# One written-out list of work replaced by another, from segment 0's attention on, on one Trainium2 core

## The chip, the core and the metric

The kernel runs on one core of one Trainium2 chip. Five engines work side by side, each through its own queue in order: TensorE (PE; its weight loads are listed as PEld), VectorE (DVE), ScalarE (ACT), GpSimd (POOL) and SyncE (SP), which here only issues DMAs. They wait for one another through semaphores. ScalarE can issue DMAs too; its transfers appear as queue q10, those of SP as q1. Both share the core's 16 DMA engines. The metric is the device time of one execution in microseconds (us).

## What is computed

Sequence 2048, width 640, 32 heads of 20, in bfloat16. A memory-augmented attention layer over 4 segments of 512 tokens, then a dense layer:

```python
for s in range(4):                              # q, k, v from layernorm(x) @ wq, wk, wv
    p = softmax(qs @ ks.T * scale + causal)     # inside the segment
    a_dot = p @ vs
    a_mem = (phi(qs) @ M) / (phi(qs) @ z + 1e-6)   # phi(t) = t + 1 if t > 0 else exp(t)
    outs.append(g * a_mem + (1 - g) * a_dot)    # g = sigmoid(beta), per head
    M, z = M + phi(ks).T @ vs, z + sum(phi(ks))
h = x + concat(outs) @ wo
out = h + silu(layernorm(h) @ w1) @ w2          # w1: 640 x 1728
```

## The kernel before

Every piece of work is a named task of a few instructions on one engine. `ORDER` is one long string that lists all tasks; nothing is decided when the program runs. Going through it, `Graph.schedule` appends each task to its engine's queue. So the string fixes three things: the order on each engine, the engine where a task has a choice (`/A` ScalarE, `/D` VectorE, `/G` GpSimd, `/S` SP; for a DMA, which queue issues it) and, behind the colon, the slot of each buffer that the task takes (for PSUM the first of its banks, 0 to 7).

```python
        for row in ORDER:
            name, _, slots = row.partition(":")
            name, _, eng = name.partition("/")
```

The waits follow from that: `Tracker.add` makes an instruction wait for the last writer and readers of what it reads and overwrites, PSUM banks and buffer slots among them. A task that gets a slot waits until its former user has been read.

The tasks, with `s` the segment (0 to 3), `b` the block of 128 tokens (0 to 15), `c` a chunk of 128 rows, `f` a chunk of the 1728 (0 to 13):

- `x`, `w_...`: loads. `w_w2_0` to `w_w2_3` are four parts of w2 (L582), which land on memory that holds segment 0's q and k until its scores are done. `x12` loads blocks 12 to 15 (L579, 640 KB) into the place of blocks 0 to 3, after these have been stored. `out{b}` stores a block (L1259).
- `n1_st`, `n1_r`, `n1_ap`, `n1_tr` and `n2_...`: layer norm statistics (L747, L750), the power for the deviation (L762 or L765, then L768), its application (L774, VectorE) and the DMA transpose of the result (L798, SP), before the attention (`n1`) and before the dense layer (`n2`).
- `pr{s}{c}{w}` (L861, PE): q (w = 0) and k (w = 1), evicted from PSUM by `qe` (L869 on ScalarE, L870 on VectorE); `ex`, `pha`, `phb` make phi (L876, L883, L889). `v{s}{i}` (L826) and `ve` (L836, L837): v. `vt`: small DMAs (L901) that gather the heads that lie across chunks.
- `qk` (L938): scores of four heads. `e` (L949, ScalarE): their exponentials, two banks each. `mk` (L960, GpSimd): the mask. `av` (L981): times v. `oe` (L994 or L996): its eviction. `tn` (L1010, L1014): the memory's part and the transposition of `oe`. `nm` (three instructions L1041 to L1047, or L1027 and L1029 in segment 0): division, reading the bank of `tn`. `ad` (L1055, GpSimd): the sum. In segments 1 to 3 the tasks of a group of four heads carry the number 8 s + g; in segment 0 `x` and `y` are the first and second half of the segment's rows.
- `kt{s}{c}` (L1095, SP): DMA transpose of phi(k) out of one of three slots of phiK into one of two of phiKt. `mz` (L1103): the update of M. `ma`, `mb` (L1129, L1132, L1139): its accumulation and masked copy.
- `ot` (L1156, SP transpose), `wo` (L1164), `rs` (L1172, VectorE): output projection. `h1_{s}_{f}` (L1199; the last chunk L1193), `th` (L1208, ScalarE), `s{s}_{f}` (L1214, VectorE): the first dense matrix and silu. `h2_{b}_{part}` (L1241), `o{b}` (L1254): the second.

The dense layer of a segment is spread between the attention tasks of the next, so TensorE has matmuls to do while exponentials are made. SP's queue is in order like the others: a transfer that waits holds all behind it.

Of the kernel before, what the change touches and what calls it, by code (L numbers as in the profile page):

```python
# [389 lines left out]
w_w2_2/S w_w2_3/S phb100 tn5y:1 e7yb0:0 e7yb2 qe140/D nm5y:1 mk7yb_0 ex121:2 mk7yb_256 pha140:0 h1_0_1_0:2 th0_1_0:1  # L390
s0_1_0 qk8a0:3 pr111:7 e8a0:2 phb121 qe111/D vt16/S:0 vt10/S tn4y:0 nm4y:3 e8a2 mk8a_0 vt19/S vt13/S h1_0_8_0:1
th0_8_0:1 ex140:0 s0_8_0 h1_0_6_0:2 th0_6_0:0 phb140 qk8e0:4 e8e0:6 s0_6_0 av6y:3 oe6y/D:0 e8e2 mk8e_0 av7y:1 mk8e_256
h1_0_10_0:0 th0_10_0:1 qk8b0:2 e8b2:4 tn6y:6 oe7y/D:1 nm6y:0 tn7y:7 nm7y:3 pr130:1 ot3 ot2 s0_10_0 e8b0 mk8b_0
mk8b_384 qk9a0:4 qe130/D:0 e9a0:0 pr131:0 qe131/D vt18/S vt14/S n1_tr8:0 vt111/S e9a2 vt15/S mk9a_0 vt11/S n1_tr10
vt12/S pha130:0 vt17/S h1_0_2_0:1 qk9b0:2 h1_0_11_0:0 th0_2_0:1 mz04:6 s0_2_0 e9b0:5 e9b2 kt12:1 ma04/D:1 pha131:1
mk9b_0 mk9b_384 n1_tr9 th0_11_0:0 mz03:7 ma03/D:4 h1_0_0_0:1 th0_0_0:1 h1_0_13_0:3 mb03:0 ex130:0 qk10a0:4 s0_11_0
s0_0_0 e10a2:3 th0_13_0:0 e10a0 mb04:0 mk10a_0 s0_13_0 h1_0_9_0:2 th0_9_0:0 s0_9_0 ex131:1 phb131 phb130 h2_0_0:0
h2_0_1 kt13:0 n1_tr11 qk10b0:3 e10b0:1 e10b2 mk10b_0 mk10b_384 ex141:1 av9:7 av8:2 oe8/D:1 oe9/D:0 h2_0_2 qk10e0:2
e10e0:4 h2_0_3 o0 pha111:0 out0/S vt110/S e10e2 mk10e_0 mk10e_256 ex110:2 h2_1_0:6 phb110 qk11a0:2 e11a0:6 wo3:0 rs3
e11a2 mk11a_0 n2_st3:1 n2_r3/G h2_1_1 qk11b0:2 e11b2:0 e11b0 mk11b_0 mk11b_384 tn8:0 nm8:2,1 h2_1_2 h2_1_3 o1 qk12a0:2  # L400
out1/S n2_ap3:0 pha141:1 n2_tr3 e12a2:5 e12a0 mk12a_0 ex111:0 phb141 ad8:0 wo2:0 rs2 av10:6 oe10/D:1 qk12b0:2 mz13:7
ma13 e12b2:2 e12b0 mk12b_0 mk12b_384 phb111 n2_st2:7 pr220:1 qe220/D:0 n2_r2/D qk13a0:4 e13a2:3 av11:0 e13a0 mk13a_0
tn9:2 v20:6 kt10:0 nm9:1,0 ad9 mz12:1 ma12 oe11/A:0 n2_ap2:2 n2_tr2 ve20/A:0 qk12e0:2 e12e0:0 mz10:0 ma10 e12e2
mk12e_0 v21:6 ve21/D qk13b0:0 e13b0:1 e13b2 mk13b_0 kt11:0 kt14:1 mk12e_256 mk13b_384 pr211:5 qe211/D:0 ex211:2
pr210:4 qk14a0:0 e14a0:4 qe210/D tn11:6 pr231:5 e14a2 mk14a_0 nm11:3,1 ad11 ex210:0 qe231/D:0 ex231:1 pr200:4 qk14b0:0
e14b0:6 qe200/D:0 pha211:2 phb211 e14b2 av13:7 oe13/D:0 v23:5 ve23/A mk14b_0 mk14b_384 h1_0_8_1:4 th0_8_1:1 s0_8_1
qk14e0:0 e14e0:1 tn13:5 nm13:3,1 pr201:7 e14e2 mk14e_0 mz11:4 mk14e_256 tn10:0 ma11 qe201/A ex200:2 nm10:0,0 ad10
pha200:0 h1_0_7_1:3 th0_7_1:0 qk15a0:4 s0_7_1 pr221:2 e15a2:3 e15a0 mk15a_0 pha201:1 phb200 av14:1 oe14/D:0 qe221/A
pha221:0 ex201:2 ad13 av12:0 qk15b0:3 vt23/S:0 vt26/S vt29/S e15b2:4 e15b0 mk15b_0 tn14:1 mb11:0 mk15b_384 oe12/D:1
nm14:3,0 ad14 mb10:0 pha210:0 phb201 pr241:7 qe241/A:0 h1_0_12_1:6 th0_12_1:1 qk16b0:0 tn12:4 s0_12_1 nm12:0,1 e16b0:2  # L410
h1_0_4_1:7 th0_4_1:0 s0_4_1 e16b2 phb210 vt20/S h1_0_0_1:6 th0_0_1:1 ad12 h1_0_10_1:0 th0_10_1:0 av15:1 oe15/A:0
s0_10_1 s0_0_1 mk16b_0 ex221:2 phb221 kt22:0 qk16a0:2 mk16b_384 e16a2:6 h1_0_6_1:7 tn15:0 mb13:0 pr240:6 nm15:0,0 ad15
ot6:0 qe240/D e16a0 th0_6_1:0 ot7 ot4 ot5 s0_6_1 mb12:0 mk16a_0 h1_0_5_1:4 th0_5_1:1 qk16e0:0 e16e0:5 s0_5_1 pr230:5
qe230/D vt22/S vt27/S vt21/S pha240:0 vt25/S pha230:0 vt28/S e16e2 mk16e_0 ex240:2 vt211/S mk16e_256 v22:6 ve22/D
pha220:0 ex230:0 qk17b0:2 e17b2:3 e17b0 mk17b_0 mk17b_384 phb230 phb240 vt210/S vt24/S h1_0_13_1:1 th0_13_1:1 pha231:0
phb231 s0_13_1 h1_0_11_1:0 th0_11_1:0 ex220:0 wo6:6 qk18b0:2 e18b0:0 rs6 e18b2 mk18b_0 mk18b_384 s0_11_1 av16:1
oe16/D:1 wo7:6 phb220 ex241:2 qk17a0:0 rs7 n2_st6:6 n2_r6/G wo4:4 rs4 e17a0:6 e17a2 mk17a_0 n2_st7:4 n2_r7/G
h1_0_3_1:7 th0_3_1:0 h1_0_9_1:6 th0_9_1:1 s0_9_1 qk18e0:0 e18e0:1 wo5:4 e18e2 mk18e_0 mk18e_256 s0_3_1 n2_ap6:2 rs5
h1_0_1_1:6 th0_1_1:0 s0_1_1 h1_0_2_1:1 th0_2_1:1 s0_2_1 n2_st4:3 n2_r4/D n2_st5:0 n2_tr6:0 n2_ap7:0 n2_tr7 n2_r5/D
# [5 lines left out]
e20a2 mk20a_0 n1_st12:0 th1_12_0:0 s1_12_0 th1_1_0:1 s1_1_0 n1_r12/G n1_ap12:1 n1_tr12:0 n1_st13:3 n1_r13/G mz23:3
kt21:1 qk20e0:4 e20e0:4 h1_1_5_0:2 ma23 e20e2 th1_5_0:1 s1_5_0 n1_st14:6 n1_r14/G n1_ap13:0 n1_tr13 mk20e_0 mk20e_256
h1_1_11_0:0 qk21a0:4 th1_11_0:0 s1_11_0 e21a2:1 h1_1_2_0:1 th1_2_0:1 s1_2_0 n1_st15:1 e21a0 mk21a_0 n1_r15/D n1_ap14:2
n1_tr14 n1_ap15:3 n1_tr15 h1_1_6_0:3 th1_6_0:0 s1_6_0 h1_1_8_0:2 th1_8_0:1 qk22a0:4 e22a2:2 e22a0 v30:0 h1_1_0_0:6
s1_8_0 av21:7 ve30/A:1 th1_0_0:0 s1_0_0 oe21/A:1 av20:5 qk22b0:1 mz21:0 ma21 e22b0:3 tn21:6 nm21:1,1 ad21 mk22a_0
e22b2 mk22b_0 mk22b_384 oe20/D:1 h1_1_9_0:0 th1_9_0:1 s1_9_0 qk23a0:1 e23a2:6 v32:6 e23a0 pr300:5 qe300/A:0 qk22e0:0  # L430
e22e0:1 ve32/D mk23a_0 e22e2 mk22e_0 mk22e_256 ex300:2 kt20:1 pha300:0 tn19:6 nm19:2,0 pr310:4 qe310/D:0 ex310:1
pr301:5 mz20:7 ma20 phb300 qk23b0:0 e23b0:0 e23b2 mb20:0 ad19 kt24:1 qe301/D mk23b_0 mk23b_384 pr311:6 h1_1_3_0:4
th1_3_0:0 qe311/D qk24e0:0 e24e2:4 tn20:5 nm20:1,1 pr320:7 e24e0 ad20 qe320/A:0 ex320:2 s1_3_0 pr330:3 qe330/D:0
av23:2 qk25a0:4 e25a2:5 e25a0 mk25a_0 ex330:0 v33:0 pr321:3 qe321/A vt33/S:0 vt36/S vt30/S vt39/S oe23/D:0 qk24b0:4
e24b0:0 ve33/D tn23:0 e24b2 mk24b_0 mb23:0 mk24b_384 nm23:1,0 ad23 mk24e_0 pha330:0 mk24e_256 phb330 pha320:0 phb320
pr341:2 qe341/A:0 av22:3 qk24a0:4 e24a0:6 e24a2 mk24a_0 oe22/D:1 pr331:1 pr340:0 qe340/A qe331/D vt37/S vt35/S vt31/S
vt34/S qk26b0:4 e26b2:1 tn22:2 nm22:3,1 ad22 mb21:0 e26b0 ot11:0 ot9 vt38/S vt310/A pha340:0 ex340:2 vt311/S ot8 ot10
vt32/S v31:0 mz24:6 qk25b0:2 ve31/D e25b0:2 ma24 e25b2 mk25b_0 mk25b_384 mk26b_0 mb24:0 mk26b_384 phb340 pha310:0
# [878 lines left out]
```

## Time and profile before

| | us |
|---|---|
| median of 3 runs (302.9 to 304.97) | 304.0 |
| the profiled execution | 303.38 |
| its span, first to last instruction | 301.7 |
| TensorE busy in the span | 290.1 |
| ScalarE, VectorE, GpSimd busy | 222.4, 219.5, 141.0 |

The profile comes from one execution, whose span lies 1.7 us under its own time. A line of the profile names the line of the kernel (L1103), the tiles written and read, and a count; lines of waits name the engine that stood, what ended the wait, its sum, count and longest. Since tasks have few lines between them, a task is found in the trace by its place in its engine's order: the n-th instruction of an engine is the n-th that the list puts there. So `kt23`, the twelfth of the 15 `kt` in SP's order, is the twelfth transpose of L1095 in the trace.

### The profile page before, as it was taken

The numbers are of one execution on the slowest core, as the hardware profiler recorded it, in microseconds if no ns is written. First come the engines' busy times: TensorE is split into PE (matmuls) and PEld (weight loads), VectorE is DVE, ScalarE is ACT, GpSimd is POOL, SyncE is SP. The second block draws the span as 40 slices with busy tenths as digits, with TensorE's granted clock in tenths as the row PEclk, the third lists the DMA queues.
The fourth block names the chain that finished last, engine by engine and source line by source line (L and its number), as shares of the span: only waits on it lengthen the run. The fifth ranks groups of instructions, "written<-read, shape, count | busy, mean of one in ns | idle before, by whom it ended". The sixth has DMA issues, their size and how long they took to land.

```text
span 301.7 us, 7526 instructions
## 1 busy us (share of the span) xinstructions
PE 290.1 (96%) x3006; PEld 173.1 (57%) x3029; DVE 219.5 (73%) x517; ACT 222.4 (74%) x317; POOL 141.0 (47%) x271
## 2 busy tenths in 40 slices
...
GB/s 249 365 340 100 110 122 111 89 78 130 81 88 94 57 2 28 54 83 37 87 128 39 72 13 20 39 77 82 49 65 24 2 43 46 74 100 2 0 30 59
DMA packets 49250, 24.66 MB, mean 82 GB/s; under 512 B 39168, under 2 KB 47616, under 8 KB 49216
## 3 DMA queue, kind: packets, MB, share of 16 engines
...
q8 instruction: 24, 0.39, 0.6%
q14 instruction: 10, 0.08, 0.1%
...
## 4 chain that ended last, share of the span: by engine, by line
PE 75%; DVE 9%; DMA 7%; ACT 6%; issue 1%; POOL 0%; ACTq 0%; DVEq 0%
PE ps_all L1241 18%; PE ps_all L1199 15%; PE ps_all L861 12%; PE ps_all L826 7%; PE ps_all L938 6%; PE ps_all L1164 6%; PE ps_all L981 5%; ACT PT L949 4%; DMA phiKt<-phiK 3%; PE ps_all L1010 2%; DMA x_tok<-in_A_x_dram 2%; DVE stt L747 2%; PE ps_all L1014 1%; DMA hT<-xn_rot 1%; PE ps_all L1103 1%
## 5 line engine op out<-in xcount | busy, mean ns | idle before, releaser
L949 ACT ACTIVATE PT<-ps_all 128x1024 bf16<-128x1024 f32 (+1 forms) x168 | 157.7, 994 | 15.9 <-PE ps_all L938 14.1
L960 POOL TENSOR_SCALAR_AFFINE_SELECT PT<-PT 128x512 bf16<-128x512 bf16 x128 | 81.2, 642 | 73.2 <-ACT PT L949 70.5
L1241 PE MATMUL ps_all<-w_sb,sT 128*128 128x320 bf16 (+2 forms) x462 | 64.8, 295 | 0.0
L1199 PE MATMUL ps_all<-hT,w_sb 128*128 128x512 bf16 (+1 forms) x315 | 61.1, 336 | 1.4 <-issue 0.7
L1208 ACT ACTIVATE th<-ps_all 128x512 f32<-128x512 f32 (+2 forms) x70 | 34.8, 520 | 36.6 <-PE ps_all L1193 21.2
L1241 PEld LDWEIGHTS ps_all<-w_sb,sT 128*128 128x128 bf16 x462 | 43.2, 98 | 18.3 <-issue 2.2
L1214 DVE SCALAR_TENSOR_TENSOR sT<-th,ps_all 128x512 bf16<-128x512 f32 (+2 forms) x70 | 37.9, 560 | 18.0 <-ACT th L1208 17.4
L1199 PEld LDWEIGHTS ps_all<-hT,w_sb 128*128 128x128 bf16 x325 | 29.7, 98 | 25.5 <-issue 2.7
L1254 DVE SCALAR_TENSOR_TENSOR x_tok<-ps_all,x_tok 128x640 bf16<-128x640 f32 (+3 forms) x18 | 13.3, 748 | 22.2 <-PE ps_all L1241 22.2
L747 DVE BATCH_NORM_STATS2 stt<-x_tok 128x6 f32<-128x320 bf16 x62 | 27.2, 480 | 1.6 <-DMA x_tok<-in_A_x_dram 1.3
L768 POOL TENSOR_TENSOR rst<-rst,eps_c 128x1 f32<-128x1 f32 x32 | 18.5, 579 | 14.0 <-DVE rst L762 12.2
L1164 PE MATMUL ps_all<-wo_sb,oT 128*128 128x320 bf16 x160 | 24.1, 299 | 0.0
L1055 POOL TENSOR_TENSOR otok<-on 128x320 bf16<-128x320 bf16 x24 | 19.5, 813 | 9.6 <-DVE on L1047 9.6
L981 PE MATMUL ps_all<-PT,Vx 128*32 128x256 bf16 (+3 forms) x576 | 23.3, 287 | 0.5 <-DVE Mz L1129 0.3
L1047 DVE TENSOR_TENSOR on<-ps_all,rd 128x640 bf16<-128x640 f32 x24 | 19.8, 824 | 0.8
L996 DVE TENSOR_SCALAR oTs<-ps_all,lsc 128x512 bf16<-128x512 f32 (+1 forms) x30 | 18.3, 620 | 2.0 <-PE ps_all L981 1.9
L1164 PEld LDWEIGHTS ps_all<-wo_sb,oT 128*128 128x128 bf16 x160 | 14.9, 98 | 7.2 <-issue 2.0
L826 PE MATMUL ps_all<-wv_sb,xT 128*128 128x320 bf16 x120 | 18.3, 299 | 0.7 <-DVE sT L1214 0.3
L981 PEld LDWEIGHTS ps_all<-PT,Vx 128*32 128x32 bf16 x576 | 12.2, 96 | 10.5 <-issue 4.7
L861 PE MATMUL ps_all<-xT,wkr 128*128 128x512 bf16 x67 | 16.9, 380 | 1.0 <-issue 0.8
L861 PE MATMUL ps_all<-xT,wqr 128*128 128x512 bf16 x70 | 17.4, 380 | 0.5 <-issue 0.3
L774 DVE TENSOR_SCALAR xn_rot<-x_tok,mvt,rst 128x640 bf16<-128x640 bf16 x32 | 13.8, 438 | 5.0 <-POOL rst L768 3.8
...
## 6 DMA issues: line engine op xcount, KB each, us to landing
...
```

The source lines that it names most:

```text
L747: T.add(DV, lambda e, hh=hh: e.bn_stats(out=stt[:, s, 6 * hh:6 * hh + 6], in_=xb[:, 320 * hh:320 * hh + 320]), reads=R((xa, xsub)), writes ...
L826: fns.append(lambda e, c=c, hh=hh: e.matmul(bank(ps, hh)[:, 0:320], lhsT=xT_[:, c, 128 * i:128 * i + 128], rhs=wv_sb[:, c, 320 * hh:320 * ...
L861: fns = [lambda e, kc=kc: e.matmul(bank(ps)[:, lo:hi], lhsT=wt[:, kc, c, :], rhs=xT_[:, kc, lo:hi], start=(kc == 0), stop=(kc == NC - 1)) ...
L949: T.add(AC, lambda e: e.activation(out=pt[:, pta.slot, q0:q0 + 2, 0:width], in_=sc3[:, b0:b0 + 2, 0:width], func=ACT.Exp, scale=SCALE), re ...
L960: T.add(PO, lambda e: e.affine_select(out=v, in_=v, pattern=[[0, 4], [1, 128]], compare_op=ALU.is_ge, fill=0.0, base=0, channel_multiplier ...
L981: fns.append(lambda e, j=j, r=r, h=h, pa=pa, pt=pt, co=co, q0=q0, ji=ji: e.matmul(bank(po)[32 * r:32 * r + 32, q0:hi], lhsT=Vx[:, vx.slot, ...
L1047: T.add(DV, lambda e: e.tensor_tensor(out=on[:, ona.slot, :, :].rearrange("p b (x e) -> p b x e", e=DH), in0=v[:, :, :, 0:DH], in1=r2.unsq ...
L1164: fns.append(lambda e, c=c, hh=hh: e.matmul(bank(ps, hh)[:, 0:320], lhsT=oT[:, c, 128 * i:128 * i + 128], rhs=wo_sb[:, c, 320 * hh:320 * h ...
L1199: fns = [lambda e, c=c: e.matmul(bank(ps)[:, lo:hi], lhsT=w1_sb[:, c, 128 * f:128 * f + 128], rhs=hT[:, c, lo:hi], start=(c == 0), stop=(c ...
L1208: T.add(AC, lambda e: e.activation(out=th[:, tha.slot, lo:hi], in_=bank(ps)[:, lo:hi], func=ACT.Tanh, scale=0.5), reads=R((ps, [0])), writ ...
L1214: T.add(DV, lambda e: e.scalar_tensor_tensor(out=sT[:, f, lo:hi], in0=th[:, tha.slot, lo:hi], scalar=1.0, in1=bank(ps)[:, lo:hi], op0=ALU. ...
L1241: fns.append(lambda e, f=f, t0=t0, fr=fr, hh=hh, n=n: e.matmul(bank(pa, hh)[:, 0:n], lhsT=sT[:, f, t0:t0 + 128], rhs=w2_sb[:, fr, c0 + 320 ...
```

## The change

The list is replaced from the task `av0y` on: the first and the last rows are shown, and those between that this text speaks of. No task is added or removed, no other line of the kernel is touched. 25 tasks change their engine or queue, among them `ve23`, `qe300`, `qe320`, `qe321`, `qe340` and `oe25` (ScalarE to VectorE), `qe330`, `qe331`, `oe24` and `oe30` (VectorE to ScalarE), and seven of the last stores (between SP and ScalarE). On TensorE about a quarter of its 410 tasks start after more or less other work than before, up to 245 us by 0.1 to 3.5 us of it; from there on whole groups change places.

The words that came with the change: the list was searched anew, with the transfers of both DMA queues counted in the order of their issue times.

```diff
-av0y:2 oe0y/D:1 mz02:3 ma02/D:3 v12:0 kt01:0 e2ya2 qk2yb0:2 e2yb0:1 ve12/D phb031 e2yb2 mk2yb_0 mk2yb_256 wo1:6 rs1
-n2_st1:5 n2_r1/G qk3ya0:0 e3ya2:3 wo0:4 mb02:0 tn0y:6 nm0y:1 e3ya0 rs0 n2_ap1:3 n2_tr1:0 av1y:7 qk4ya0:0 oe1y/D:0
-pr101:6 qe101/D:0 n2_st0:3 n2_r0/G v13:4 ve13/D e4ya2:4 w_w2_0/A e4ya0 pha101:2 ex101:2 phb101 n2_ap0:3 qk3yb0:0
...
-s0_12_0 av5y:6 mb01:0 e7ya0 h1_0_4_0:7 th0_4_0:0 s0_5_0 oe5y/D:0 qk6yb0:3 e6yb2:5 e6yb0 mk6yb_0 mk6yb_256 pr110:0
-h1_0_3_0:2 th0_3_0:1 tn3y:1 s0_4_0 kt03:0 qe110/D:0 pha110:0 nm3y:0 s0_3_0 ex100:1 av4y:7 oe4y/D:1 qk7yb0:3 pr140:0
...
-qk20b0:2 e20b0:5 mk19a_0 av19:6 oe18/D:0 tn18:0 h1_1_10_0:7 e20b2 mk20b_0 mk20b_384 nm18:2,0 mz14:2
-ma14 kt23:1 mb14:0 oe19/A:0 th1_10_0:0 ad18 s1_10_0:0 qk21b0:3 x12/A tn16:0 h1_1_7_0:2 h1_1_4_0:7 nm16:2,1 e21b2:6
+av0y:2 oe0y/D:1 mz02:3 ma02/D:3 v12:0 kt01:0 e2ya2 qk2yb0:2 e2yb0:1 ve12/D phb031 w_w2_0/A e2yb2 mk2yb_0 mb02:0
+mk2yb_256 wo1:6 qk3ya0:0 e3ya2:3 wo0:4 e3ya0 rs1 n2_st1:5 n2_r1/G tn0y:6 nm0y:1 rs0 n2_ap1:3 n2_tr1:0 av1y:7 qk4ya0:0
...
+oe5y/D:1 mz01:7 ma01/D:2 mb01:0 kt03:0 tn3y:0 nm3y:0 e7ya0 h1_0_4_0:1 qk6yb0:4 e6yb0:5 pr110:0 qe110/D:0 e6yb2 mk6yb_0
...
+o0 out0/S pha111:0 n1_tr8 mk10e_0 mk10e_256 ex111:2 phb111 h2_1_0:6 phb110 qk11a0:2 e11a2:6 wo3:0 e11a0 mk11a_0 tn8:4
+rs3 nm8:2,1 ad8:0 ex141:1 n2_st3:1 pha141:1 n2_r3/D h2_1_1 qk11b0:0 e11b2:0 e11b0 mk11b_0 mk11b_384 h2_1_2 h2_1_3 o1
...
+mk14b_0 av13:7 qe200/D:0 ex200:2 v23:4 h1_0_8_1:6 mk14a_0 oe13/D:0 ve23/D mk14b_384 th0_8_1:1 qk14e0:0 s0_8_1 mz11:7
+e14e2:1 tn13:4 e14e0 ma11 pr201:6 nm13:3,1 qe201/A mk14e_0 mk14e_256 tn10:2 nm10:0,0 ad10 pha200:0 h1_0_7_1:0
...
+qk20b0:3 e20b2:5 out3/S mk19a_0 av19:2 oe18/D:0 tn18:0 mz14:7 e20b0 nm18:2,0 ad18 h1_1_10_0:6 ma14 mk20b_0 mb14:0
+kt23:1 mk20b_384 oe19/A:0 th1_10_0:0 s1_10_0:0 tn16:4 qk21b0:0 x12/A nm16:2,1 h1_1_4_0:7 ad16 e21b0:6 e21b2 pha241:0
+h1_1_7_0:6 th1_4_0:0 s1_4_0 th1_7_0:1 s1_7_0 mk21b_0 phb241 qk20a0:2 e20a2:0 h1_1_1_0:0 e20a0 n1_st12:0 h1_1_12_0:1
+th1_1_0:1 s1_1_0 mk20a_0 th1_12_0:0 s1_12_0 n1_r12/G n1_ap12:1 n1_tr12:0 n1_st13:3 n1_r13/G qk20e0:4 h1_1_5_0:2
...
+h2_15_0_0:0 h2_15_1_0 h2_15_2_0 h2_15_3_0 o15_0 out15_0/S h2_15_2_2 h2_15_3_2 o15_2 out15_2/A
```

More of the change, by code (lines that the diff above doesn't have):

```diff
@@ L390 @@
[L390 to L419, printed above, removed]
@@ L425 @@
[L425 to L438, printed above, removed]
-phb310 h1_1_13_0:7 h2_4_0:0 h2_4_1 qk26a0:2 th1_13_0:0 s1_13_0 e26a2:3 h2_4_2 h2_4_3 av25:6 av24:7 e26a0 mk26a_0 o4
@@ new lines @@
+e4ya0:4 oe1y/D:0 pr101:6 qe101/D:0 v13:4 e4ya2 n2_st0:3 ve13/D pha101:2 ex101:2 n2_r0/G n2_ap0:3 n2_tr0 qk3yb0:0
+e3yb2:5 pr120:7 qe120/D:0 phb101 pha120:0 e3yb0 mk3yb_0 qk4yb0:2 e4yb0:0 w_w2_1/S e4yb2 mk4yb_0 mk4yb_256 mk3yb_256
+ex120:0 av2y:6 oe2y/D:1 pr100:0 qe100/D qk5ya0:2 e5ya2:2 tn2y:6 nm2y:2 pr121:1 qe121/D e5ya0 qk5yb0:4 e5yb0:6 phb120
+pha121:0 n1_ap8:3 pr141:0 e5yb2 mk5yb_0 qk6ya0:1 qe141/D:0 h1_0_7_0:5 tn1y:7 nm1y:1 e6ya0:1 th0_7_0:0 av3y:6 oe3y/D:1
+mk5yb_256 s0_7_0:0 pha100:0 e6ya2 h1_0_12_0:0 th0_12_0:0 s0_12_0 h1_0_5_0:1 th0_5_0:1 qk7ya0:2 e7ya2:3 s0_5_0 av5y:6
```

97 lines of the change are left out of this document (66 added, 31 removed).

## Prediction

> **What bounds the kernel now.** I read the page's first part, then busy time in stretches of one stage each, then TensorE's waits from 43 us on, where the two lists part, and then the DMA queues at the two largest of them.
>
> ```profile
> PE 290.1 (96%) x3006; PEld 173.1 (57%) x3029; DVE 219.5 (73%) x517; ACT 222.4 (74%) x317; POOL 141.0 (47%) x271
> ```
> ```profile
> 43.00:75.00 32.00, 29.94 (x365) 16.44 (x363) 26.72 (x67) 30.00 (x44) 12.71 (x22) 1.00 0.39 98
> 75.00:100.00 25.00, 24.63 (x295) 14.98 (x294) 17.54 (x41) 23.04 (x32) 13.99 (x23) 1.00 0.50 83
> 100.00:150.00 50.00, 49.62 (x564) 29.57 (x560) 40.14 (x94) 45.26 (x65) 28.79 (x46) 1.00 0.27 52
> 150.00:174.00 24.00, 21.91 (x206) 10.17 (x202) 19.00 (x45) 21.20 (x29) 10.13 (x18) 1.00 0.39 79
> 174.00:269.00 95.00, 93.78 (x935) 55.70 (x939) 66.58 (x132) 59.68 (x76) 43.95 (x71) 1.00 0.24 48
> ```
> The columns of the stretches are start:end, length, then busy us of PE, PEld, DVE, ACT and POOL, the granted clock, DMA share and GB/s. TensorE is full (49.62 of 50 us) except in the first and the fourth stretch, and the clock is 1.00 throughout. From 43 to 75 us ScalarE is as full as TensorE (30.00 against 29.94 of 32). Both lists hold the same matmuls, so a list can only take away TensorE's idle time, or add to it. This is that idle time from 43 us on:
>
> ```profile
> PE ps_all L861 <- issue: 1.1, 7, 0.2
> PE ps_all L1014 <- DVE oTs L996: 0.9, 1, 0.9
> PE ps_all L1199 <- issue: 0.7, 4, 0.2
> PE ps_all L938 <- DVE sT L1214: 0.5, 1, 0.5
> PE ps_all L1014 <- ACT PT L949: 0.4, 1, 0.4
> PE ps_all L1103 <- DMA phiKt<-phiK: 0.4, 1, 0.4
> PE ps_all L1199 <- DVE sT L1214: 0.3, 1, 0.3
> PE ps_all L1010 <- DVE x_tok L1254: 0.3, 1, 0.3
> PE ps_all L826 <- DVE sT L1214: 0.3, 1, 0.3
> ```
> The 1.8 us put down to "issue" are not waits: in the timeline each stands beside a group of 4 matmuls where the code has 5, a missing record. The others sum to 3.1 us, and gaps too short for this view add some 0.5. So **3.6 us, 1.2%, is all that a new list can gain**; nothing but judgement of the new waits bounds the loss.
>
> Two places make up most of it. At 54.6 us `tn2y` (L1014) waits 0.9 for `oe2y`; VectorE is late there because `n2_ap0` (L774) stood 0.84 us for a transpose, issued at 48.32 by SP and landed 4.17 us later, where the median of that line is 2.6. From 158 to 167 us four waits (0.4, 0.46, 0.34, 0.25: 1.45 us) follow from `kt23`, issued at 152.76 and landed 6.0 us later (median 2.5), for which `pha241` held VectorE 2.35 us. At both, ScalarE's queue (q10) had a 640 KB load under way: `w_w2_0`, issued at 47.51, and `x12`, issued at 152.34. The queues in the DMA view (packets, MB, share of 16 engines), first for 153 to 156 us, where no other queue is listed, then for 156 to 159:
>
> ```profile
> q10 hardware_dynamic: 411, 0.53, 66.6%
> ```
> ```profile
> q1 hardware_dynamic: 544, 0.13, 57.5%
> q10 hardware_dynamic: 117, 0.13, 11.9%
> ```
> The reader is to see that SP's queue q1 moves nothing in the first three us, though `kt23` was issued before them; its 0.13 MB flow when the load is nearly over. From 48.5 to 51 us it is the same: 484 packets of q10 and none of q1. A transpose behind a large load of the other queue waits for nearly all of it.
>
> **The change, part by part.**
>
> *`w_w2_0`* goes from behind `e4ya2` to behind `e2yb0` on ScalarE, which started at 43.26. It waits for what `e2yb0` waits for (`qk2yb0`), so it holds nothing; its issue (0.38 us of ScalarE's sequencer) is the same. With its 4.4 us to landing it is through at about 47.9, before `n2_tr1` goes out at 48.32. That transpose then lands at 48.32 + 2.6 = 50.9, `n2_ap0` waits for its own `n2_r0` instead (51.33), and the instructions up to `oe2y` (0.45 + 0.68 + 0.43 + 0.47, less overlaps, then 0.47) end near 53.7, when TensorE is there. The 0.85 us go. But ScalarE is full to 75 us: of its idle time in 53 to 60 us only 0.38, 0.12 and 0.11 can close, and at 72 us TensorE waits for an exponential (the 0.4 of L1014 <- L949), which no edit moves. Gain between 0 and 0.85; I take **0.4**, nearer to ScalarE's 0.6 less the next item.
>
> *Order within 55 to 73 us.* `tn3y` moves 2.5 us forward, next to `pr110`, which uses the same PSUM bank 0; `nm3y` (0.56 us) must empty it, behind `oe5y` and `ma01` on VectorE. By the rows' durations `nm3y` ends about 0.25 us after TensorE is ready for `pr110`. That wait is new; it costs nothing at 72 us as long as ScalarE is the later one, and is why I took 0.4.
>
> *`kt23` and `x12`.* `mz14` now precedes `h1_1_10_0`, so `kt23`, which waits for it (the slot of phiKt), goes out 1.03 us earlier, near 151.7; `x12`, dispatched behind `th1_10_0`, goes out some 0.45 later, near 152.8. The order of the two issues turns round. `kt23` should land by 151.7 + 2.5 = 154.2, before VectorE comes to `pha241` (end of `nm16`, 155.3). `mz23` is 1.6 us of TensorE work later as well. VectorE is then held by `n1_st12`, which needs `x12`: 152.8 + 4.4 (the other 640 KB load) to 5.9 (its own landing now) is 157.2 to 158.7, against 160.08 now. VectorE gains 1.4 to 2; of TensorE's 1.45, I take **1.2**; ends 0 and 1.45.
>
> *SP's order in 69 to 92 us.* SP issues without a pause there. `n1_tr8` goes from 77.58 to behind `out0`, last of its four. The transfers ahead of it end near 88.4, so it lands at about 91 to 93; `pr220`, its first reader, starts at 95.51. `kt12` goes out some 0.8 earlier. Nothing, unless it lands 2.5 us late.
>
> *`ex111`, `ex141`, `ve23`, `qe300` to `qe340`.* `ex141` (0.71) fills the 0.67 us in which ScalarE waits at 89 us, and `ex111` leaves a place where ScalarE would then wait for `qk12b0`: zero. `ve23` (0.71) goes to VectorE, into its 1.34 us of idle time before `s0_8_1`; `tn13`, now on the same banks, comes about 0.5 us after it. Of six evictions in 176 to 195 us four go to VectorE and two to ScalarE; `qe340` there ends just when `v31` wants its bank (195.27 against 195.28), as `qe331` does now. Zero, cover thin.
>
> *The end* (from 245 us) moves most, by up to 7.6 us, but TensorE runs through either order: its waits from 269 us are none, ScalarE has 7.71 busy of 33 us. The last two stores change queues; both queues issue one in 0.33 us. Zero.
>
> *New waits elsewhere*, not visible in this trace: from 0 to the 1.1 us that the present list has outside the two places (0.4, 0.3 and some short ones); I take **0.3**, the low side, since most neighbours keep their order.
>
> Sum: -0.4 - 1.2 + 0.3 = **-1.3 us**. The profiled execution took 303.38 us (span 301.7), so 302.1; it lies 0.6 under the median of 304.0, where the same step gives **302.7**.
>
> **A rule that speaks against it.** The Trainium skill, "DMA: Bandwidth & Descriptors", section "Queues, rings and completion order", says that a DMA engine takes turns between queues, a packet at a time, so that a small transfer would not stand behind a large one. The trace disagrees: 411 packets of q10 and none of q1. By that rule the order of issue would matter less; see the third rival.
>
> **Rivals.**
> 1. *ScalarE and `x12` take it all back.* In favour: ScalarE has 30.00 of 32 us. Against: it has 2.8 us idle in 150 to 174. Gains 0: 304.0 to 304.3.
> 2. *Slower: `x12` holds VectorE.* `n1_st12` stands ahead of `s1_1_0`, which frees bank 0 for `h1_1_11_0`. It decides from a landing of 160.08, today's start of `n1_st12`. If `x12` now stands behind `kt23` as `kt23` stood behind it (6.0 - 2.5 = 3.5 us), it lands at 152.8 + 5.9 + 3.5 = 162.2 and the place costs 2.1 more than now: -0.4 + 0.3 + 2.1 = +2.0, 306.0; with half of the 3.5, +0.3, 304.3. Against: the transpose is 0.13 MB and done in 1.3 us once it flows.
> 3. *The queues share.* Then `kt23` loses time to `x12` in either order and lands near 156, the second gain halves: -0.7, 303.3.
> 4. *Nearly all waits go*, 3.1 of the 3.6: 300.9.
>
> **Chances.** Forecast 0.48 (own range 301.4 to 303.6), rival 1 0.17, rival 2 with other new waits 0.17, rival 3 0.08, rival 4 0.10. The range 300.5 to 305.6 leaves out half of rivals 4 and 2 and the tails. Three runs of before spread over 302.9 to 304.97, so about 1% (3 us) is what can be told from no change. Faster by over 1%: most of rival 4 and a tail, 0.14. Slower: the far half of rival 2 and unseen waits, 0.12. Within 1%: 0.74.
>
> **What would show it.** `kt23` landing in about 2.5 us and no wait of L883 for it; `n2_tr1` near 48 us landing in 2.6 us and L1014 <- L996 gone; the busy share of PE in 150 to 174 us over 23 of 24. Wrong, if L747 or L1199 wait for `x12`, if L861 waits on L1029 or on a transpose near 95 us, or if ScalarE's wait at 72 us has grown by what was gained at 54.

## Result and the profile after

Over 20 runs each the changed list takes 302.73 us (301.38 to 304.21) and the list before 304.34 us (302.9 to 307.91): a ratio over the runs of **0.9955, 95% interval 0.9936 to 0.9974**, or 1.4 us (the medians alone differ by 1.6). A second set of 12 runs gave 0.9935 (0.9912 to 0.9959). The profiled execution took 301.38 us (span 299.6).

First the page's busy line of after, then its stretches, with the columns as before:

```profile
PE 289.6 (97%) x3006; PEld 172.9 (58%) x3029; DVE 221.9 (74%) x517; ACT 221.3 (74%) x315; POOL 141.1 (47%) x273
```
```profile
43.00:75.00 32.00, 30.89 (x372) 16.86 (x376) 26.53 (x70) 30.92 (x46) 13.37 (x24) 1.00 0.42 102
75.00:100.00 25.00, 24.26 (x287) 14.79 (x287) 17.80 (x41) 22.50 (x31) 13.65 (x22) 1.00 0.43 79
100.00:150.00 50.00, 49.15 (x555) 29.02 (x560) 40.73 (x91) 44.05 (x63) 28.75 (x47) 1.00 0.27 51
150.00:174.00 24.00, 23.34 (x211) 11.57 (x216) 20.24 (x46) 23.16 (x31) 12.62 (x22) 1.00 0.39 79
```
TensorE gained 0.95 us of busy time in the first stretch and 1.43 in the fourth (23.34 of 24), and lost 0.37 and 0.47 in the second and third. TensorE's waits from 43 us on, in after:

```profile
PE ps_all L861 <- issue: 0.7, 4, 0.2
PE ps_all L1103 <- DMA phiKt<-phiK: 0.4, 1, 0.4
PE ps_all L1199 <- issue: 0.4, 2, 0.2
PE ps_all L1014 <- DVE oTs L996: 0.3, 1, 0.3
PE ps_all L938 <- DVE on L1047: 0.3, 1, 0.3
PE ps_all L861 <- DVE otok L1029: 0.2, 1, 0.2
PE ps_all L1010 <- DVE x_tok L1254: 0.2, 1, 0.2
PE ps_all L1010 <- ACT oTs L994: 0.2, 1, 0.2
...
```
The 0.9 of L1014 at 54.6 us is gone (the 0.3 under that name stands at 70.9 us, for another tile), and so are the 0.5 of L938, the 0.4 of L1103 and the 0.3 of L1199 between 155 and 168 us. New are another 0.4 of L1103, for the transpose `kt10` at 98 us, and a handful of 0.2 to 0.3. The reason for what went is in the DMA view of after, first from 42 to 49 us, then from 151 to 158 us (bytes, then us from issue to landing; the first of the two `phiKt` is `kt01`, the second `kt23`):

```profile
w_sb<-in_B_w_dram ACTq DMA_DIRECT2D x1, 640.0 KB, 4.2
phiKt<-phiK SPq DMA_TRANSPOSE x1, 2.4
hT<-xn_rot SPq DMA_TRANSPOSE x1, 2.6
```
```profile
x_tok<-in_A_x_dram ACTq DMA_DIRECT2D x1, 640.0 KB, 5.3
phiKt<-phiK SPq DMA_TRANSPOSE x1, 2.4
```
`n2_tr1` lands in 2.6 us where it took 4.17, `kt23` in 2.4 where it took 6.0. The queues of after from 152 to 154 us, and then from 155 to 158 us, where one queue alone is listed:

```profile
q1 hardware_dynamic: 544, 0.13, 33.1%
q10 hardware_dynamic: 18, 0.02, 15.8%
```
```profile
q10 hardware_dynamic: 416, 0.51, 47.4%
```
It is the picture of before turned round: the 544 packets of the transpose go first, the load behind them.

**Where the time went, by place.** The two lists hold the same tasks, so the start of a `qk` (or of `av0y`, `v20`) on TensorE can be laid beside its start in the profile of before. The table gives that difference in us. Up to `av0y` all these lists are the same; the last column is therefore what the list does from there on, without the spread of the start.

| run | av0y (40.6 in before) | qk6ya0 (57.3) | v20 (98.0) | qk16a0 (122.0) | qk17a0 (133.4) | qk19a0 (145.9) | qk21a0 (163.0) | last task | av0y to the end |
|---|---|---|---|---|---|---|---|---|---|
| after | -0.33 | -1.06 | -1.30 | -0.82 | -0.21 | -0.15 | -1.95 | -2.00 | -1.67 |
| after_again | 0.56 | -0.17 | -0.58 | -0.65 | -0.04 | 0.02 | -1.65 | -1.57 | -2.13 |
| b_w2 | 1.60 | 0.87 | 0.66 | 0.66 | 0.67 | 1.05 | 1.05 | 1.05 | -0.55 |
| b_x12sp | 0.03 | 0.03 | -0.18 | -0.18 | -0.17 | -0.17 | -1.12 | -1.13 | -1.16 |
| b_two | 1.21 | 0.48 | 0.27 | 0.27 | 0.27 | 0.27 | -1.30 | -1.28 | -2.49 |
| b_two_again | 0.23 | -0.50 | -0.71 | -0.71 | -0.71 | -0.62 | -1.63 | -1.61 | -1.84 |
| a_w2back | 2.68 | 3.45 | 3.25 | 3.43 | 4.05 | 4.11 | 2.79 | 2.87 | 0.19 |
| a_mz14back | -0.02 | -0.75 | -1.21 | -1.27 | -0.66 | -0.60 | 1.64 | 1.30 | 1.32 |
| a_mz14back_again | 1.33 | 0.59 | 0.29 | 0.23 | 0.84 | 0.91 | 1.11 | 1.20 | -0.13 |
| a_mz10 | 2.26 | 1.53 | 1.31 | 1.22 | 1.83 | 1.89 | 0.43 | 0.50 | -1.76 |
| a_mid | 0.88 | 0.15 | -0.20 | -0.27 | 0.34 | 0.34 | -0.89 | -0.81 | -1.69 |

For after: -0.73 at 54 us, -0.24 to 98 us, +0.48 to 122 us, +0.61 to 133 us, +0.06, **-1.80** to 163 us, -0.05 from there to the end.

### The profile page after: what moved, and what is told of

Its sections match the earlier page's. It is cut to its first block, busy times and chain, and to the rows that moved or that the text cites. A ratio compares the mean times of both kernels' runs of the same rounds, so it can differ in the third digit from the quotient of the medians.

```text
span 299.6 us, 7538 instructions
## 1 busy us (share of the span) xinstructions
PE 289.6 (97%) x3006; PEld 172.9 (58%) x3029; DVE 221.9 (74%) x517; ACT 221.3 (74%) x315; POOL 141.1 (47%) x273
## 3 DMA queue, kind: packets, MB, share of 16 engines
HBM read 10.41 MB, written 2.62 MB: 43 GB/s over the span
## 4 chain that ended last, share of the span: by engine, by line
PE 79%; DVE 10%; DMA 6%; ACT 3%; issue 1%; POOL 0%; DVEq 0%; ACTq 0%
PE ps_all L1241 20%; PE ps_all L1199 14%; PE ps_all L861 13%; PE ps_all L1164 7%; PE ps_all L938 7%; PE ps_all L826 7%; PE ps_all L981 5%; DMA phiKt<-phiK 3%; DMA x_tok<-in_A_x_dram 3%; PE ps_all L1103 2%; DVE stt L747 2%; DVE on L1047 2%; ACT PT L949 2%; PE ps_all L1010 2%; PE ps_all L1014 1%
## 5 line engine op out<-in xcount | busy, mean ns | idle before, releaser
L1199 PE MATMUL ps_all<-hT,w_sb 128*128 128x512 bf16 (+1 forms) x315 | 61.0, 336 | 1.0 <-issue 0.4
L1199 PEld LDWEIGHTS ps_all<-hT,w_sb 128*128 128x128 bf16 x325 | 29.8, 98 | 25.2 <-issue 2.3
L747 DVE BATCH_NORM_STATS2 stt<-x_tok 128x6 f32<-128x320 bf16 x62 | 27.2, 480 | 1.9 <-DMA x_tok<-in_A_x_dram 1.6
L870 DVE CAST QK<-ps_all 128x512 bf16<-128x512 f32 x24 | 16.4, 685 | 5.4 <-PE ps_all L861 5.2
L996 DVE TENSOR_SCALAR oTs<-ps_all,lsc 128x512 bf16<-128x512 f32 (+1 forms) x29 | 17.7, 616 | 1.9 <-PE ps_all L981 1.6
L861 PE MATMUL ps_all<-xT,wqr 128*128 128x512 bf16 x69 | 17.2, 380 | 0.7 <-DVE otok L1029 0.2
L861 PE MATMUL ps_all<-xT,wkr 128*128 128x512 bf16 x68 | 17.2, 380 | 0.7 <-issue 0.5
```

What stands on the lines that cost most here:

```text
L747: T.add(DV, lambda e, hh=hh: e.bn_stats(out=stt[:, s, 6 * hh:6 * hh + 6], in_=xb[:, 320 * hh:320 * hh + 320]), reads=R((xa, xsub)), writes ...
L861: fns = [lambda e, kc=kc: e.matmul(bank(ps)[:, lo:hi], lhsT=wt[:, kc, c, :], rhs=xT_[:, kc, lo:hi], start=(kc == 0), stop=(kc == NC - 1)) ...
L1199: fns = [lambda e, c=c: e.matmul(bank(ps)[:, lo:hi], lhsT=w1_sb[:, c, 128 * f:128 * f + 128], rhs=hT[:, c, lo:hi], start=(c == 0), stop=(c ...
```

## The experiments

Names with b_ start from the list before, names with a_ from the list after. Rests of a row that don't matter are left out.

### The first place alone (b_w2)

```diff
-ve12/D phb031 e2yb2 mk2yb_0
-ve13/D e4ya2:4 w_w2_0/A e4ya0
+ve12/D phb031 w_w2_0/A e2yb2 mk2yb_0
+ve13/D e4ya2:4 e4ya0
```


> The list of before with one entry moved: w_w2_0 behind e2yb0, as the changed list has it. Theory A (a transpose waits for a load that the other queue issued ahead of it): n2_tr1 lands in about 2.6 us instead of 4.2, VectorE's wait of 0.84 before n2_ap0 goes, TensorE's 0.85 before tn2y goes, and 0.4 to 0.9 us of the span stay gained: 303.4 to 303.9 where before has 304.3. Rival B (the other moves of the list made the gain): n2_tr1 may land early, but ScalarE is full until 75 us, and the time stays within 0.2 us of before.

Ratio **0.9958 (0.9937 to 0.998)**; `n2_tr1` lands in 2.62 us, and TensorE gains the same 0.73 us between `av0y` and `qk6ya0` as in after (1.60 to 0.87). TensorE's waits of b_w2 from 43 to 75 us, then the longest from 148 to 175 us:

```profile
PE ps_all L1014 <- ACT PT L949: 0.4, 1, 0.4
```
```profile
PE ps_all L938 <- DVE sT L1214: 0.7, 1, 0.7
```
At 54 us nothing is left; around 160 us it is as before, since `kt23` (issued 153.81, behind `x12` at 153.39) lands in 5.76 us. So the moved issue alone makes the first gain, and none of the reordering around it is needed. From `av0y` to the end the run gains 0.55: before `qk19a0` 0.38 are lost again, where TensorE waits 0.3 us for `ot4`, which lands in 5.44 us, met by an instruction packet (see a_fill20).

### The second place alone, by the queue (b_x12sp)

`x12` is put on SP's own queue behind `kt23`, so that it can't be ahead of it:

```diff
-ma14 kt23:1 mb14:0 oe19/A:0 th1_10_0:0 ad18 s1_10_0:0 qk21b0:3 x12/A tn16:0
+ma14 kt23:1 x12/S mb14:0 oe19/A:0 th1_10_0:0 ad18 s1_10_0:0 qk21b0:3 tn16:0
```


> The list of before with one entry moved: x12 is issued by SP, directly behind kt23, instead of by ScalarE at nearly the same moment. Theory A: kt23 goes first and lands in about 2.5 us, pha241 no longer holds VectorE, x12 lands about 1.5 us later than before (near 159 to 160), and 0.7 to 1.5 us are gained: 302.8 to 303.6 where before has 304.3. Rival (the queues share the DMA engines by turns, so who is first does not matter): kt23 gains little, as x12 is still under way beside or behind it, and the time stays within 0.3 us of before. Rival (VectorE is only held one step later, by n1_st12 for x12): kt23 early, but TensorE's waits in 158 to 167 us stay above 1 us.

Ratio **0.9964 (0.9934 to 0.9993)**. Its DMA view from 152 to 155 us:

```profile
x_tok<-in_A_x_dram SPq DMA_DIRECT2D x1, 640.0 KB, 5.1
phiKt<-phiK SPq DMA_TRANSPOSE x1, 3.6
```
`kt23` lands in 3.6 us instead of 6.0 and TensorE gains 0.95 us at this place, somewhat over half of what after gains. No task of TensorE was moved, so it is the order of the two transfers that pays, not the new order of matmuls. It does not land in the 2.5 us that were expected, though nothing large is ahead of it: its first packet moves 1.18 us behind the issue as in after, but a packet of 16 KB of another queue, named instruction (q8), starts 1.17 us behind the issue. More on these packets below. VectorE then waits 1.4 us for `x12`, which goes second here.

### Less load ahead of the transpose (b_x12quarter)

The order is that of before, with `x12` still first, but it loads only block 12: the loads of blocks 13 to 15 are left out.

```diff
-            lambda e: e.dma_start(out=x_tok[:, s0:s0 + n, :], in_=xv[:, b0:b0 + n, :]), prio, bw, kind, engs=engs)
+            lambda e, m=1 if b0 == 12 else n: e.dma_start(out=x_tok[:, s0:s0 + m, :], in_=xv[:, b0:b0 + m, :]), prio, bw, kind, engs=engs)
```


> The kernel before, with x12 loading block 12 alone, 160 KB instead of 640 (blocks 13 to 15 are then computed from what lies there). Theory A (kt23 waits until the load ahead of it is over): kt23 lands 1.2 us or more earlier than its 6.0, at 3.5 to 4.8, as 480 KB less at 400 GB/s are ahead of it. Rival (taking turns): kt23 was slowed by something other than the load's length, and lands within 0.5 us of 6.0, or it had only to share and lands near 2.6.

`kt23`, 0.43 us behind it, lands in 3.89 us (6.01 behind the whole), and TensorE gains 1.6 us between `qk19a0` and `qk21a0` against before; one execution took 301.84 us beside 304.81 of before. What the load costs is best read from the first packet of the transpose. It moves 1.18 us behind the issue in after (no load ahead), 1.29 here and 3.41 in before; at that moment 119 of the quarter load's 144 packets and 464 of the whole load's 528 have started. So the transpose waits until the load is nearly over, less for less: 0.1 us here, 2.2 us in before.

The rest of both landings has another cause. The view of before from 156 to 159 us, of which the prediction shows q1 and q10, has a third row, and so has that of this run from 152 to 157 us:

```profile
q8 instruction: 1, 0.02, 2.0%
```
```profile
q8 instruction: 1, 0.02, 1.5%
```
This packet starts 1.16 us behind the issue of `kt23` here; `kt12`, with no load ahead of it and such a packet 1.16 us behind its issue, takes 3.63 us in after_again. In before it starts at 156.29, just as the transpose begins to move, and the transpose takes 2.6 us from its first packet to the landing, instead of 1.2 in after. So of the 3.6 us by which `kt23` is later in before than in after, about 2.2 are the load and the rest is probably the instruction packet, which the earlier issue escapes as well.

### Each place taken back (a_w2back, a_mz14back)

```diff
-ve12/D phb031 w_w2_0/A e2yb2
-v13:4 e4ya2 n2_st0:3
+ve12/D phb031 e2yb2
+v13:4 e4ya2 w_w2_0/A n2_st0:3
```


> The changed list with w_w2_0 put back behind e4ya2. Theory A: n2_tr1 lands late again (about 4.2 us), TensorE waits 0.5 to 0.9 us for oe2y near 54 us, and the time is 0.4 to 0.9 us over the changed kernel: a ratio to before of 0.997 to 0.999 instead of 0.9955. Rival B (the other moves): no difference from the changed kernel beyond 0.2 us.

Ratio 0.9974 (0.9944 to 1.0003), an interval that overlaps that of after, so the times alone show no loss; the trace does. `n2_tr1` takes 4.27 us again, and TensorE's only wait of a_w2back between 43 and 75 us is this one:

```profile
PE ps_all L1014 <- DVE oTs L996: 1.6, 1, 1.6
```
It is longer than the 0.9 of before: from `av0y` to `qk6ya0` this run loses 0.77 against before where after gains 0.73, a swing of 1.5. In this profile the list after needs the early load more than the list before did.

```diff
-tn18:0 mz14:7 e20b0 nm18:2,0 ad18 h1_1_10_0:6 ma14
+tn18:0 e20b0 nm18:2,0 ad18 h1_1_10_0:6 mz14:7 ma14
```


> The changed list with mz14 put back behind h1_1_10_0, so that kt23 goes out some 1 us later and x12 some 0.45 us earlier, at nearly the same moment again. Theory A: kt23 lands in about 6 us again, VectorE waits 2 us or more for it before pha241, TensorE waits 1.2 to 1.9 us in 155 to 167 us, and most of the 1.85 us gained there is lost: a ratio to before of 0.999 to 1.001. Rival (the gain came from mz23 standing 1.6 us later and from the order of th1 and s1): kt23 lands late, yet less than 0.6 us is lost.

Ratio **1.0027 (0.9997 to 1.0057)**: one matrix update put behind one group of dense matmuls takes away the whole gain. `kt23` (152.47) stands behind `x12` (152.05) again and lands in 5.66 us. VectorE's and TensorE's longest waits of a_mz14back from 148 to 175 us:

```profile
DVE phiK L883 <- DMA phiKt<-phiK: 3.3, 1, 3.3
```
```profile
PE ps_all L938 <- DVE sT L1214: 2.0, 1, 2.0
```
But from `qk20a0` (155.8 us) to `qk21a0` TensorE loses 2.12 us against before (-0.48 to 1.64) where after gains 1.61 (-0.34 to -1.95): a swing of 3.7 us, more than that wait. The stretches of this profile from 159 us on show the rest (the number behind the counts of POOL is the granted clock):

```profile
159.00:160.00 1.00, 0.01 (x4) 0.02 (x5) 1.00 (x3) 0.00 (x0) 0.00 (x0) 1.00 0.00 0
160.00:161.00 1.00, 1.00 (x12) 0.43 (x13) 1.00 (x3) 0.99 (x3) 0.00 (x0) 1.00 0.00 0
161.00:162.00 1.00, 1.00 (x6) 0.54 (x5) 0.97 (x4) 1.00 (x3) 0.53 (x2) 0.65 0.00 0
162.00:163.00 1.00, 1.00 (x5) 0.54 (x4) 1.00 (x3) 1.00 (x3) 0.21 (x1) 0.50 0.00 0
163.00:164.00 1.00, 1.00 (x3) 0.30 (x2) 0.96 (x4) 0.42 (x1) 0.07 (x1) 0.50 0.00 0
164.00:165.00 1.00, 1.00 (x7) 0.15 (x6) 1.00 (x3) 0.19 (x1) 0.92 (x3) 0.65 0.82 164
```
TensorE stood from 157.9 to 160.0 us; 1.3 us later the clock is 0.50 for 3.4 us, and TensorE looks full while it does half the work. That loses 0.35 + 0.50 + 0.50 + 0.35 = 1.7 us, which with the 2.0 of waiting makes the 3.7. To see whether the clock belongs to the list, the same kernel ran once more:

> The list after with mz14 behind h1_1_10_0 again, unchanged from the earlier run of it, whose profile showed, behind a wait of TensorE of 2.0 us from 158.0 to 160.0 us, a granted clock of 0.50 from about 161.3 to 164.7 us, which no other profile of this case has. The loss there of 3.7 us against the list after is then 2.0 of waiting and 1.7 of half clock. Theory A, the fall of the clock follows from the standstill: kt23 lands in 5.6 to 6 us again, TensorE waits 1.8 to 2.2 us, the clock is about half for some 3 us behind it, and the ratio is 1.000 to 1.006 again. Theory B, the fall was chance of that one execution: the same wait, but a clock of 1.00 throughout, and the half clock can't be part of the median's loss. Theory C, the wait itself was chance: kt23 lands in 2.4 to 4 us, no wait above 1 us, ratio near 0.995.

Ratio 1.0022 (0.9986 to 1.0057); `kt23` lands in 5.4 us. TensorE's longest wait of a_mz14back_again from 148 to 175 us:

```profile
PE ps_all L938 <- DVE sT L1214: 1.5, 1, 1.5
```
In this execution the clock stays at 1.00, and from `qk20a0` to `qk21a0` it needs 0.09 us more than before (1.02 to 1.11), so **1.7 us more than after, which is what the order of `kt23` and `x12` is worth without the clock** in these two profiles. The mean granted clock of each timed run tells how often it falls: 0.006 under full is 1.8 us over 303. It was 0.994 in 7 of 12 runs of the first set and in 2 of 10 of the second; in the 32 runs of after never, in the 12 of a_mz10 once, in the 94 of before that have a clock on record once. So neither theory A nor B holds as written: the fall comes far more often in the list with the long wait, but not each time, and not in that list alone.

### The two places together, and nothing else (b_two, b_two_again)

The list before with the edit of b_w2, and with the rows from `out3` to `mk20e_256` (64 tasks around `kt23`) as in after:

```diff
-qk20b0:2 e20b0:5 mk19a_0 av19:6 oe18/D:0 tn18:0 h1_1_10_0:7 e20b2
-mk20b_0 mk20b_384 nm18:2,0 mz14:2
...
+qk20b0:3 e20b2:5 out3/S mk19a_0 av19:2 oe18/D:0 tn18:0 mz14:7 e20b0
+nm18:2,0 ad18 h1_1_10_0:6 ma14 mk20b_0 mb14:0
...
```


> The list of before with two pieces of the changed list alone: w_w2_0 behind e2yb0, and the stretch from out3 to mk20e_256 (149 to 160 us: mz14 ahead of h1_1_10_0, so kt23 out about 1 us ahead of x12, and mz23 later). All else as before. Theory A: this is all of the gain. Stage times of the runs so far give -0.7 for the first and -1.85 for the second: -2.3 to -2.6, ratio 0.991 to 0.993, below the changed kernel's 0.9955, because the rest of the changed list costs some 0.5 to 1 us (its new waits at 98 and 122 to 126 us). Rival B (the rest of the list gains too): ratio 0.996 to 0.998, above the changed kernel's.

Ratio **0.991 (0.988 to 0.994)**, from 6 runs: 301.75 us against 304.81. TensorE's stage times show -0.73 at the first place, -0.21 behind it, 0.00 all the way from 98 to 146 us, -1.57 at the second, and nothing else. Run again beside another set:

> The list of before with the two pieces of the changed list, as in b_two: ratio 0.988 to 0.994 again, -2.5 us from av0y to the end. Theory (the rest of the changed list costs): below the changed kernel's ratio, and equal to a_mid's within 0.2 us.

Ratio 0.9942 (0.9916 to 0.9969). The two sets of this kernel and the two of after overlap, so the two edits alone can't be told from the whole new list; nothing of the rest is needed for the gain, and that the rest costs something, as expected, isn't shown by the times. In this second profile the margin failed, and from `av0y` to the end it gains 1.84 instead of the expected 2.5. Its DMA view from 151 to 154 us, then its queues from 154 to 157 us:

```profile
q1 hardware_dynamic: 512, 0.13, 26.1%
q10 hardware_dynamic: 42, 0.05, 17.0%
q8 instruction: 1, 0.02, 1.8%
...
phiKt<-phiK SPq DMA_TRANSPOSE x1, 5.6
```
```profile
q10 hardware_dynamic: 486, 0.60, 55.9%
q1 hardware_dynamic: 32, 0.00, 0.6%
```
`kt23` was issued at 151.06, 1.09 us ahead of `x12`, which in the other profiles with this order (after, b_two, after_again, a_mid among them) was enough for 2.42 or 2.43. Here the 16 KB packet of the instruction queue (q8) ran from about 0.5 us after the issue for 0.88 us; 512 of the 544 packets went in time, and the last 32 only when the load was through. TensorE's gain at the place fell to 1.01.

### The new wait for `kt10` (a_mz10, after_again)

`mz10`, which reads `kt10`, is put behind `mz12`:

```diff
-v20:6 mz10:0 ma10 ad9
-mz12:1 ma12 v21:6
+v20:6 ad9
+mz12:1 ma12 mz10:0 ma10 v21:6
```


> The changed list with mz10 put back behind mz12. Its wait of 0.37 for kt10 at 98.6 us goes, whatever made kt10 late there (it landed 4.27 us after its issue, directly behind the store out1 and with a 16 KB instruction load on queue q8 1.9 us after its issue): 0.2 to 0.4 us under the changed kernel, ratio 0.994 to 0.995. If another wait takes its place (for ma12 or ve21), no difference.

> The changed kernel as it is, on the same chip as the others of this group: ratio 0.9936 to 0.9974 as before. TensorE's stage times should show the gain between av0y and the end again, near 1.7 us, and the spread between executions in the first 40 us, where both lists are the same.

a_mz10: 0.9926 (0.9902 to 0.9949). `kt10` is late there (3.97 us), and yet from `v20` to `qk16a0` TensorE loses nothing (-0.09, where after lost 0.48): the cover works. after_again, unchanged, loses nothing either (-0.07), for `kt10` lands in 2.43 there. SP's order is the same in both, with `out1` just ahead of `kt10`, so that is not what delays it. The queues of after from 96.2 to 97.2 us and from 97.2 to 98.8 us, with `kt10` issued at 94.28:

```profile
q8 instruction: 1, 0.02, 7.7%
q1 hardware_dynamic: 11, 0.00, 0.6%
```
```profile
q1 hardware_dynamic: 2, 0.00, 0.2%
```
Nearly all of the transpose's packets have gone when the 16 KB packet starts, 1.9 us after the issue; it takes 1.23 us, and the last two packets of the transpose follow it. In after_again it starts 2.3 us after, when none is left. The wait is real in the profiled execution, and there or not by 0.3 us.

### When the instruction packet comes (a_fill20)

The first row of the list keeps TensorE busy with 36 filler matmuls while the first loads arrive. With 16 fewer, all that follows on TensorE stands at another place of its instruction stream:

```diff
-fill36:0
+fill20:0
```


> The changed kernel with 20 instead of 36 of the filler matmuls that TensorE runs on zeros in the first 7 us. Theory (a 16 KB instruction load on queue q8 that comes 1.8 to 2.3 us after a transpose's issue delays its landing from 2.6 to about 4.2 us, and the loads come as TensorE uses up its instructions): all loads come 16 matmuls later, 2 to 4 us on; ot5, n2_tr6 and kt12, late in every profile so far, then land in about 2.6 us, unless another load meets them, and other transposes are late instead. Rival (these transposes are late for what stands ahead of them in SP's queue): they stay late, at 3.6 to 4.4.

One execution took 300.43 us beside a median of 304.46 for before; a single time can't tell that from a good start. What it does tell: `kt12`, which took 4.47 us in before and 4.08 in after, each time with a q8 packet 2.05 us behind its issue, lands in 2.43; the packet now comes 3.8 us behind. The DMA view from 82 to 85 us, of after and then of a_fill20:

```profile
q8 instruction: 1, 0.02, 2.0%
phiKt<-phiK SPq DMA_TRANSPOSE x1, 4.1
```
```profile
q1 hardware_dynamic: 597, 0.20, 35.5%
phiKt<-phiK SPq DMA_TRANSPOSE x1, 2.4
```
`n2_tr6` and `n1_tr6` come on time too (2.58 and 2.69), `n1_tr10` is late instead (3.84). `ot5` stays late (4.37), with a packet 2.18 us behind its issue. The packets follow TensorE's count of instructions: each profile has 24 of them, one for about 250 matmuls and weight loads, and the one that meets `kt12` starts after 1974, 1974 and 1973 of these in before, after and a_fill20 (others vary by up to some 50). So the late transposes move with the instruction packets. Not all of these three were late in every earlier profile, as the expectation has it: with the packet a little later, 2.21 and 2.31 us behind the issue, `kt12` took 2.44 us in a_mz14back and `n2_tr6` 2.57 in a_w2back.

### The 0.61 us at 122 to 133 us (a_mid)

After with the rows from behind `qk15b0` (112 us) to `o3` (148 us) as they were in before:

```diff
-av12:0 qk15b0:3 e15b2:4 vt29/S:0 e15b0 mk15b_0 tn14:1
...
+av12:0 qk15b0:3 vt23/S:0 vt26/S vt29/S e15b2:4 e15b0 mk15b_0 tn14:1
...
```


> The changed list with the stretch from behind qk15b0 to o3 (116 to 150 us) put back to that of before; ahead of it and behind it the changed list. In five profiles of lists that hold the changed stretch, 0.6 us is lost between qk16a0 and qk17a0 (122 to 133 us), whatever else was edited; in lists with the old stretch nothing. Theory (the changed order there costs it: oe15 and nm15 late, TensorE's 0.18 and 0.28): the loss goes, -2.3 to -2.6 from av0y to the end, ratio 0.990 to 0.993. Rival (it is paid back later, as TensorE then runs into another wait): no more than 0.2 us better than the changed kernel.

Ratio 0.9961 (0.9931 to 0.999). The loss is still 0.61 (-0.27 to 0.34), and TensorE's waits from 115 to 140 us are the same two as in after:

```profile
PE ps_all L938 <- DVE on L1047: 0.3, 1, 0.3
PE ps_all L1010 <- ACT oTs L994: 0.2, 1, 0.2
```
So the order of this stretch is not the cause. Followed task by task, before, b_two, after and a_mid agree within 0.01 us up to `th0_0_1`; then ScalarE stands 0.2 us before `th0_10_1` in after, after_again and a_mid, with no wait that the profile shows, and not in before or b_two. `oe15` and `tn15` are 0.28 late by it. VectorE's `phb221` then starts just behind GpSimd's mask instead of ahead of it. The timeline of VectorE, of after and then of b_two:

```profile
122.81 0.87 DVE L889 TENSOR_TENSOR phiK<-phiK,ex 128x512 bf16<-128x512 bf16 x1 [0.34 <-ACT ex L876]
```
```profile
123.62 0.44 DVE L889 TENSOR_TENSOR phiK<-phiK,ex 128x512 bf16<-128x512 bf16 x1 [0.34 <-ACT ex L876]
```
In after GpSimd's `mk16b_384` runs from 122.77 to 123.40, so it has begun 0.04 us earlier; in b_two it begins at 123.86, 0.24 later. Together, 0.28 and 0.43, less a small overlap, make `nm15` 0.67 late, and `qk16e0`, which wants its bank, 0.61. The Trainium skill, "SBUF — State Buffer", section "Who interferes with whom", says that a VectorE operation on two tensors in SBUF contends with GpSimd's reads, and that the one which begins first keeps the port: these two rows agree (0.44 against 0.87), though standing until the mask's end at 123.40 and then running 0.44 would make it 1.03. What makes ScalarE stand 0.2 us before `th0_10_1` stays open.

## Why the prediction was right

The forecast was 302.7 us and within 1%; 302.73 was measured. The mechanism was right; that the number came out to 0.03 us is luck. By the trace of after the two places gave -0.73 and -1.80 where -0.4 and -1.2 were forecast, and the rest of the list cost +0.86 where +0.3 was; and the forecast stood on a median of before of 304.0 from 3 runs, where 20 runs have 304.34.

- **What bounds the kernel.** Right: TensorE's idle time was all there was to gain, and two places made up most of it. No run gained more than 2.5 us of the 3.6 between `av0y` and the end, but for the one execution with fewer fillers (2.8).
- **`w_w2_0`: mis-sized.** Forecast -0.4, measured -0.73 in after and b_w2, near the upper end (0.85). `n2_tr1` landed at 50.55 (forecast 50.9). The step that failed is that ScalarE, 30.00 of 32 us busy, would take half of it back: its share rose to 30.92, and the 0.73 were kept to 98 us.
- **Order within 55 to 73 us.** Right: L861 waits 0.24 us on L1029 for `pr110`, forecast 0.25; it did not cost, since `qk9a0` at 73.6 us is 0.91 earlier than `av0y` let expect. The prediction also has this wait among its signs of being wrong; by its own step it is none.
- **`kt23` and `x12`: mis-sized, and one wait left out.** Forecast -1.2, measured -1.80 and -1.67 in the two profiles of after and -1.57 in b_two, but -1.46, -1.32 and -1.23 in a_mz10, a_w2back and a_mid, which have the same order at this place. The upper end of 1.45 was passed, as it counted only the four waits that the trace of before listed. The times came out: `kt23` issued 151.53 and landed 153.96 (forecast 151.7 and 154.2), `x12` issued 152.63 and landed 157.97 (152.8 and 157.2 to 158.7). VectorE's waits of after from 148 to 175 us have no line of L883 for a DMA any more, but this:

```profile
DVE stt L747 <- DMA x_tok<-in_A_x_dram: 0.6, 1, 0.6
```
  The prediction named a wait of L747 for `x12` as a sign of being wrong, and its second rival had the chain: `n1_st12` stands ahead of `s1_1_0`, which frees the bank of `h1_1_11_0`. That chain is real and sets the size of the gain. `x12` takes 5.34 us in after and then, in after_again, b_two, a_mz10, a_w2back and a_mid, 5.60, 5.69, 5.81, 5.95 and 6.04; from 5.60 on each tenth more takes a tenth off the gain (1.67, 1.57, 1.46, 1.32, 1.23). In a_mid from 148 to 175 us the wait of VectorE and that of TensorE behind it are:

```profile
DVE stt L747 <- DMA x_tok<-in_A_x_dram: 1.3, 1, 1.3
```
```profile
PE ps_all L1199 <- DVE sT L1214: 0.4, 1, 0.4
```
  In a_fill20 `x12` lands in 4.20, VectorE doesn't wait for it, and the gain is 1.81, no more than in after. So this rival had the mechanism right and the size wrong: it costs up to 0.6 us of the 1.8. It reckoned from 160.08 as if a landing before that were free.
- **SP's order: wrong in part.** `n1_tr8` landed at 91.8 (forecast 91 to 93) at no cost. But "nothing" did not hold for `kt10`, 0.37 us of waiting in the profiled execution; the prediction's clause, a landing late by about 2.5 us, met it at 1.9. The cause, an instruction packet, was not among its reasons.
- **`ex`, `ve`, `qe` and the end.** Right from `qk21a0` to the last task: -0.05 in after, +0.08 in after_again and a_mid. Earlier, where `ex111`, `ex141` and `ve23` stand, no run takes these alone.
- **New waits.** Forecast +0.3. With what the places gave, after has -1.67 + 0.73 + 1.80 = +0.86, after_again -2.13 + 0.73 + 1.67 = +0.27, both within the 0 to 1.1 that it gave as the range. Most of the difference is `kt10`; both hold the 0.61 of 122 to 133 us.
- **Rivals.** ScalarE did not take it back. `x12` was not held for 3.5 us behind `kt23`; the 3.5 itself was the load for about 2.2 and probably the instruction packet for the rest. The queues don't share: no packet of q1 moves until the load ahead of it is nearly over (464 of 528 packets started), and the same in b_x12quarter with a shorter load (119 of 144); the rule of the Trainium skill that the prediction weighed ("DMA: Bandwidth & Descriptors", "Queues, rings and completion order") is not what these transfers do. Nearly all waits (3.1 us) did not go.

The 0.6 by which the profiled execution of before lay under its median is probably the start: at `av0y`, with one and the same list up to there, the profiles lie from -0.33 to +2.68 us, a spread of 3.0 us, where the 20 runs of after spread over 2.8. What makes the start differ was not followed.
